# Pass two of a gated spectral/GEGLU training step: accumulators by halves, scratch in blocks, gate gradient as columns, last row tile half by half

## The chip, the cores and the metric

One core of a Trainium2 chip. The metric is the device time of one execution in microseconds (us), lower is better. Each kernel was run several times in rounds in which kernels alternate on the same chip; medians are quoted. A ratio is the mean time of one kernel's fast runs over that of the other's fast runs of the same rounds, so it is not quite the ratio of the medians beside it. "Same" means within 2%.

## The reference, cut to what matters

```python
def _fwd_reference(A_x, A_w_r, A_w_i, B_x, B_w_gate, B_w_up, B_w_down, gate_w):
    x = A_x                                              # [1, 2048, 576] bf16
    g = _sigmoid((x * gate_w).sum(-1, keepdims=True))
    a = _A_ref(x, A_w_r, A_w_i)                          # irfft2(rfft2(x) * W)
    b = _B_ref(x, B_w_gate, B_w_up, B_w_down)            # (gelu(x@wg) * (x@wu)) @ wd, F = 4608
    return g * a + (1 - g) * b
# reference(): this output and, by vjp with grad_out, the gradients of x, w_r, w_i, w_gate, w_up, w_down, gate_w
```

Pass one of the kernel runs the FFTs as matmuls, forms the hidden activation A and its two gradients dHg and dHu, the weight gradients, and stores A, dHg and dHu to scratch in DRAM. Pass two reads the scratch back transposed and contracts over F = 4608, in 36 chunks of 128: a "b" job makes one row tile of the FFN output from A and w_down; a "g" and a "u" job together make one row tile of the input gradient from dHg, w_gate, dHu and w_up. There are 16 row tiles, so 48 jobs of 72 matmuls.

## The kernel before

The parts that matter here (cuts marked with "..."):

```python
scr = [[dram.tile([TPB, P, FF], BF16, name=f"scr{k}_{tp}") for tp in range(NT)] for k in range(3)]
# pass one stores 128 rows of 256 elements at a row pitch of 4608 elements
LD.dma_start(scr[k][tp][:, :, fsl].rearrange("t p f -> p t f"), tl[:])
...
p2in = ctx.enter_context(tc.tile_pool(name="p2in", bufs=6, side="right", **kw))
def pin(k, t, f0):                       # one transposing DMA: 128 rows x 1536 columns; three per job
    tl = p2in.tile([P, FCB, P], BF16, tag="pin", name="pin")
    LD.dma_start_transpose(tl[:], scr[k][t // TPB][t % TPB][:, f0 * P:(f0 + FCB) * P])
    return tl

jobs = [("g", t) for t in range(3)] + [("b", t) for t in range(8)] + [("u", t) for t in range(3)] + [("b", 8)]
for t in range(3, T):
    jobs += [("g", t), ("u", t)] + ([("b", t + 6)] if t + 6 < T else [])
...
tc.tile_pool(name="pacc", bufs=4, space=PSUM, **kw) as pacc      # four accumulators of two banks
def b_job(t):
    bps = pacc.tile([P, 2, 512], F32, tag="acc", name="acc")
    ...
    for f0 in range(0, NFC, FCB):
        At = loaded.pop((0, t, f0))
        for r in range(FCB):
            fc = f0 + r
            for h in range(2):
                nc.tensor.matmul(bps[:, h, :288], lhsT=At[:, r, :], rhs=wd_all[:, fc, h * 288:(h + 1) * 288],
                                 start=(fc == 0), stop=(fc == NFC - 1))
        used[0] += 1
        ensure()                          # issues the next pin, six ahead
    nc.scalar.copy(bo[:].rearrange("p (h d) -> p h d", h=2), bps[:, :, :288])
    ...
def gate_grad():                          # 32 matmuls of 288 columns, one useful row
    for h in range(2):
        for t in range(T):
            nc.tensor.matmul(gps[:, h, :288], lhsT=dlog_bc[:, t, :], rhs=xn[:, t, h * 288:(h + 1) * 288], ...)
def x_end(t):
    ...
    nc.scalar.copy(xo[:].rearrange("p (h d) -> p h d", h=2), xps[:, :, :288])
    V.scalar_tensor_tensor(t1_[:], gwf[:], dlog[:, t:t + 1], xo[:], op0=ALU.mult, op1=ALU.add)
    V.tensor_tensor(o1[:], t1_[:], dxa_t[:], op=ALU.add)
    ST.dma_start(o1v[:, t, :], o1[:])     # ST is the POOL queue, LD the SP queue
for i, (kind, t) in enumerate(jobs):
    if i > 1 and wT_loads:
        load_wuT(*wT_loads.pop(0))        # six transposing loads of w_up, one per job from the third on
```

## Time and profile before

| | value | where from |
|---|---|---|
| time | 1493.64 us median (1491.71 to 1495.65, 4 runs) | runs |
| span of the profiled run | 1490.4 us | page |
| TensorE busy | 97% | page, part 1 |
| pass two, first matmul to last | 1045.33 to 1483.51 us | timeline of TensorE |
| lost between the first b job and the first u job | 10.75 us of 81.31 | timeline of TensorE |
| from the last matmul to the end | 6.9 us | timeline |

The profile lines stand in the prediction.

### The profile page before, as it was taken

The page shows a single profiled execution, that of the slowest core. Times are in us where ns is not written, and L with a number is a line of the kernel's source. Part 1 is how long each engine was busy: PE and PEld are TensorE (multiplying, and loading weights), DVE is VectorE, ACT ScalarE, POOL GpSimd, SP SyncE. Part 2 cuts the span into 40 slices and gives each one's busy share as a digit, 9 for nine tenths or more (in the row PEclk, how much of TensorE's full clock was granted, in tenths as well). Part 3 has the DMA queues.
Part 4 walks back from the last instruction along what each step waited for, and adds up shares of the span by engine and source line. Part 5 has one row for each costly group of instructions (what it writes and reads, how often), then busy time and mean ns, then how long its engine had stood idle before and what let it go on. Part 6 is the DMA issues. An engine that isn't in the chain of part 4 may idle for free.

```text
span 1490.4 us, 29909 instructions
## 1 busy us (share of the span) xinstructions
PE 1450.0 (97%) x11760; PEld 1071.2 (72%) x11760; DVE 843.6 (57%) x2243; ACT 698.2 (47%) x1355; POOL 22.3 (1%) x51
## 2 busy tenths in 40 slices
PE   7889999899999999999999999999998999999998
PEld 5657776666777677677677677778876777777776
DVE  7597766878888887776776776773023211212001
ACT  5576666567667766676666666662000000000000
POOL 1000000000000000000000000000000000000000
PEclk9999999999999999999999999999999999999999
DMA  5144334535444535443444544657999977878772
GB/s 187 42 136 120 91 113 143 148 106 149 135 136 130 147 104 145 128 117 110 128 117 117 149 116 117 163 133 184 245 214 213 187 156 167 162 157 171 150 153 63
DMA packets 503355, 210.49 MB, mean 141 GB/s; under 512 B 307595, under 2 KB 497068, under 8 KB 503212
## 3 DMA queue, kind: packets, MB, share of 16 engines
q1 hardware_dynamic: 499772, 202.83, 55.5%
q0 software_dynamic: 1632, 4.72, 1.2%
q8 instruction: 92, 1.51, 0.5%
q10 hardware_dynamic: 1808, 1.02, 0.2%
q14 instruction: 51, 0.42, 0.1%
HBM read 40.89 MB, written 93.82 MB: 90 GB/s over the span
## 4 chain that ended last, share of the span: by engine, by line
PE 66%; issue 23%; DVE 2%; SPq 1%; ACT 1%; DMA 1%; POOL 1%; POOLq 0%; ACTq 0%; DVEq 0%
PE wps L432 16%; PE xy L332 16%; PE wps L415 9%; PE z L320 8%; PE acc L914 3%; PE wps L445 2%; PE xy L327 2%; PE acc L956 2%; PE pf L671 2%; PE z L323 1%; PE pf L659 1%; PE pf L482 1%; POOL out_dram L971 1%; POOL out_dram L924 0%; DMA scr_p<-Vt 0%
## 5 line engine op out<-in xcount | busy, mean ns | idle before, releaser
L332 PE MATMUL xy<-wgu,xT 128*128 128x512 bf16 x1152 | 271.5, 380 | 0.0
L956 PEld LDWEIGHTS <-pin 128*128 128x128 bf16 x2304 | 225.4, 98 | 56.8
L432 PEld LDWEIGHTS <-xn 128*128 128x128 bf16 x2304 | 225.4, 98 | 32.4 <-issue 0.2
L332 PEld LDWEIGHTS <-xT 128*128 128x128 bf16 x1152 | 106.9, 98 | 137.9 <-issue 31.0
L345 ACT ACTIVATE da<-z,omg 128x256 bf16<-128x256 f32 x288 | 113.0, 475 | 154.1 <-PE z L323 154.0
L415 PE MATMUL wps<-dB,A 128*128 128x288 bf16 x1152 | 154.2, 286 | 0.0
L914 PE MATMUL acc<-wd_all,pin 128*128 128x288 bf16 x1152 | 145.4, 288 | 7.9 <-DMA pin<-scr 4.2
L320 PE MATMUL z<-wdT,dOT 128*128 128x256 bf16 x1152 | 140.2, 276 | 5.9 <-ACT Vt L622 4.1
L956 PE MATMUL acc<-wuT,pin 128*128 128x288 bf16 x1152 | 143.4, 286 | 0.0
L956 PE MATMUL acc<-wgT,pin 128*128 128x288 bf16 x1152 | 143.4, 286 | 0.0
L914 PEld LDWEIGHTS <-pin 128*128 128x128 bf16 x1152 | 113.3, 98 | 38.6 <-DMA pin<-scr 4.8
L415 PEld LDWEIGHTS <-A 128*128 128x128 bf16 x1152 | 112.7, 98 | 35.7
L432 PE MATMUL wps<-dHg,xn 128*128 128x256 bf16 x1152 | 134.4, 273 | 0.0
L432 PE MATMUL wps<-dHu,xn 128*128 128x256 bf16 x1152 | 131.5, 273 | 0.0
L320 PEld LDWEIGHTS <-dOT 128*128 128x128 bf16 x1152 | 112.6, 99 | 24.2 <-issue 9.6
L966 ACT COPY f32t<-acc 128x576 f32<-128x576 f32 x16 | 10.2, 639 | 249.1 <-PE acc L956 249.1
L351 ACT ACTIVATE q<-xy 128x512 bf16<-128x512 f32 x144 | 86.0, 597 | 73.0 <-PE xy L332 69.4
L968 DVE SCALAR_TENSOR_TENSOR f32t<-gwf,dlog,f32t 128x576 f32<-128x576 f32 x16 | 13.1, 818 | 186.9 <-ACT f32t L966 186.9
L358 DVE TENSOR_SCALAR s<-q 128x512 bf16<-128x512 bf16 x144 | 41.8, 290 | 107.9 <-ACT q L351 106.1
L367 ACT ACTIVATE om<-s 128x512 bf16<-128x512 bf16 x144 | 92.1, 640 | 6.9 <-DVE s L359 6.6
L368 ACT ACTIVATE s<-s 128x512 bf16<-128x512 bf16 x144 | 90.7, 630 | 4.6
L919 ACT COPY f32t<-acc 128x576 f32<-128x576 f32 x16 | 10.2, 640 | 172.0 <-PE acc L914 172.0
(176 smaller groups left out, 1819.8 us busy)
## 6 DMA issues: line engine op xcount, KB each, us to landing
scr<-A SPq DMA_DIRECT2D x144, 128.0 KB, 1.8
scr<-dHg SPq DMA_DIRECT2D x144, 128.0 KB, 1.9
scr<-dHu SPq DMA_DIRECT2D x144, 128.0 KB, 1.9
out_dram<-dw SPq DMA_DIRECT2D x67, 128.0 KB, 1.9
wd_all<-in_B_w_down_dram SPq DMA_DIRECT2D x3, 1728.0 KB, 12.0
out_dram<-dwd SPq DMA_DIRECT2D x34, 144.0 KB, 1.9
scr_p<-Vt SPq DMA_DIRECT2D x32, 144.5 KB, 2.3
Vp<-scr_p SPq DMA_DIRECT2D x16, 289.0 KB, 3.2
```

Source lines behind the costliest of these rows:

```text
L320: nc.tensor.matmul(zo(t), lhsT=dOT[:, ci, t, :], rhs=wdT[:, ci, :], start=(t % 4 < 2 and ci == 0), stop=False)
L327: nc.tensor.matmul(xy[t % 4 // 2][:, t % 2, :], lhsT=xT[r, 4, t, :], rhs=wgu[r, 4, :], start=True, stop=False)
L332: nc.tensor.matmul(xy[k][:, t % 2, :], lhsT=xT[:, ci, t, :], rhs=wgu[:, ci, :], start=False, stop=(ci == 3))
L345: nc.scalar.activation(da[:, tt, :], z[:, tt, k, :], ACT.Copy, scale=omg32[:, t:t + 1])
L351: nc.scalar.activation(q[:], xy[:, :, 0:FG], ACT.Square)
L358: V.tensor_scalar(s[:], q[:], A_GELU, 1.0, op0=ALU.mult, op1=ALU.add)
L367: nc.scalar.activation(om[:], s[:], ACT.Sigmoid, scale=-2.0 * C_GELU)
L368: nc.scalar.activation(s[:], s[:], ACT.Sigmoid, scale=2.0 * C_GELU)
L415: nc.tensor.matmul(wps[:, :288], lhsT=tl(0, t)[:, fch * P:(fch + 1) * P], rhs=dB[:, t, h * 288:(h + 1) * 288], start=(t == 0), stop=(t == ...
L432: nc.tensor.matmul(wps[:, cc, :], lhsT=xn[:, t, (c0 + cc) * P:(c0 + cc + 1) * P], rhs=tl(k, t), start=(t == 0), stop=(t == T - 1))
L914: nc.tensor.matmul(bps[:, h, :288], lhsT=At[:, r, :], rhs=wd_all[:, fc, h * 288:(h + 1) * 288], start=(fc == 0), stop=(fc == NFC - 1))
L956: nc.tensor.matmul(xps[:, h, :288], lhsT=src[:, r, :], rhs=wT[:, h * 288:(h + 1) * 288], start=(k == 1 and f0 + r == 0), stop=(k == 2 and ...
```

## The change

Four parts. Accumulators become single PSUM banks (eight of them), with the two halves of D one after the other, so that one half is copied out while the other is computed. The scratch is stored in blocks of 128 x 256 that a transposing DMA reads as one contiguous run. The gate gradient is made as columns: 80 matmuls with one column each. The last row tile is done half by half, the first half stored beside the second half's matmuls, from the SP queue.

```diff
-    scr = ... dram.tile([TPB, P, FF], BF16, ...)
+    scr = ... dram.tile([TPB, NG, P, FG], BF16, ...)
-            LD.dma_start(scr[k][tp][:, :, fsl].rearrange("t p f -> p t f"), tl[:])
+            LD.dma_start(scr[k][tp][:, g].rearrange("t p f -> p t f"), tl[:])
...
+        tl = p2in.tile([P, FCH, FCB // FCH, P], BF16, tag="pin", name="pin")
+        src = scr[k][t // TPB][t % TPB, g0:g0 + FCB // FCH].rearrange("g p f -> (g p) f")
+        LD.dma_start_transpose(tl[:].rearrange("q c g p -> q c (g p)"), src)
...
-         tc.tile_pool(name="pacc", bufs=4, space=PSUM, **kw) as pacc:
+         tc.tile_pool(name="pacc", bufs=8, space=PSUM, **kw) as pacc:
...
+                for h in range(2):
+                    block(bps[h], h, At, lambda r: wd_all[:, f0 + r], f0 == 0, f0 + FCB == NFC)
+                    if f0 + FCB == NFC:
+                        nc.scalar.copy(bo[:, h * 288:(h + 1) * 288], bps[h][:, :288])
...
+            for c in range(5):
+                n = min(P, D - c * P)
                 for t in range(T):
+                    nc.tensor.matmul(gps[0:n, c:c + 1], lhsT=xn[:, t, c * P:c * P + n], rhs=dlog_bf[:, t:t + 1], ...)
...
+                ST.dma_start(out_7[0:512].rearrange("(c p) -> p c", p=P), dgw[:, 0:4])
+                ST.dma_start(out_7[512:D].rearrange("(p o) -> p o", o=1), dgw[LO, 4:5])
...
+        def x_last(t):
+            ...
+            for h in range(2):
+                for k, f0, src in srcs:
+                    block(accs[t][h], h, src, wT(k, f0), k == 1 and f0 == 0, k == 2 and f0 + FCB == NFC)
+                x_out(t, h, pre, o1, LD)      # one DVE add out of PSUM, store from SP
```

More of the change, by code (lines that the diff above doesn't have):

```diff
@@ L198 @@
     o5v = out_5[0:512, :].rearrange("(c p) f -> p c f", p=P)
-    scr = [[dram.tile([TPB, P, FF], BF16, name=f"scr{k}_{tp}") for tp in range(NT)] for k in range(3)]
+    scr = [[dram.tile([TPB, NG, P, FG], BF16, name=f"scr{k}_{tp}") for tp in range(NT)] for k in range(3)]
     a_scr = dram.tile([S, D], BF16, name="a_scr")
@@ L379, in H_ew2 @@
         V.tensor_tensor(dHu[:], da[:], xb[:], op=ALU.mult)
-        fsl = slice(g * FG, (g + 1) * FG)
         for k, tl in enumerate((A, dHg, dHu)):
-            LD.dma_start(scr[k][tp][:, :, fsl].rearrange("t p f -> p t f"), tl[:])
+            LD.dma_start(scr[k][tp][:, g].rearrange("t p f -> p t f"), tl[:])
         kept.setdefault(g, []).append((A, dHg, dHu))
@@ L850, in pin @@
     def pin(k, t, f0):
-        tl = p2in.tile([P, FCB, P], BF16, tag="pin", name="pin")
-        LD.dma_start_transpose(tl[:], scr[k][t // TPB][t % TPB][:, f0 * P:(f0 + FCB) * P])
+        tl = p2in.tile([P, FCH, FCB // FCH, P], BF16, tag="pin", name="pin")
+        g0 = f0 // FCH
+        src = scr[k][t // TPB][t % TPB, g0:g0 + FCB // FCH].rearrange("g p f -> (g p) f")
+        LD.dma_start_transpose(tl[:].rearrange("q c g p -> q c (g p)"), src)
         return tl
@@ L857 @@
         jobs += [("g", t), ("u", t)] + ([("b", t + 6)] if t + 6 < T else [])
-    seq = [("bgu".index(kind), t, f0) for kind, t in jobs for f0 in range(0, NFC, FCB)]
+    jobs[-2:] = [("x", T - 1)]
+    seq = [(k, t, f0) for kind, t in jobs for k in ((1, 2) if kind == "x" else ("bgu".index(kind),)) for f0 in range(0, NFC, FCB)]
     loaded = {}
@@ L888 @@
          tc.tile_pool(name="p2res", bufs=1, **kw) as p2res, \
-         tc.tile_pool(name="pacc", bufs=4, space=PSUM, **kw) as pacc:
+         tc.tile_pool(name="pacc", bufs=8, space=PSUM, **kw) as pacc:
         wuT = [p2res.tile([P, FCB, D], BF16, name=f"wuT{k}") for k in range(NB)]
         dlog = p2res.tile([P, T], F32, name="dlog")
-        dlog_bc = p2res.tile([P, T, P], BF16, name="dlog_bc")
+        dlog_bf = p2res.tile([P, T], BF16, name="dlog_bf")
         gwf = p2res.tile([P, D], F32, name="gwf")
@@ L901, in b16t, with acc_pair, block, wT @@
             return p2b.tile([P, D], BF16, tag="b16t", name="b16t")
+        def acc_pair():
+            return [pacc.tile([P, 512], F32, tag="acc", name="acc") for _ in range(2)]
+        def block(acc, h, src, w_of, first, last):
+            for r in range(FCB):
+                nc.tensor.matmul(acc[:, :288], lhsT=src[:, r % FCH, r // FCH, :], rhs=w_of(r)[:, h * 288:(h + 1) * 288],
+                                 start=(first and r == 0), stop=(last and r == FCB - 1))
+        def wT(k, f0):
+            return (lambda r: wgT_all[f0 + r]) if k == 1 else (lambda r: wuT[f0 // FCB][:, r])
         def b_job(t):
-            bps = pacc.tile([P, 2, 512], F32, tag="acc", name="acc")
+            bps = acc_pair()
             a_t = b16t()
@@ L908, in b_job @@
             LD.dma_start(do_t[:], do_v[:, t, :])
+            bo = f32t()
             for f0 in range(0, NFC, FCB):
                 At = loaded.pop((0, t, f0))
-                for r in range(FCB):
-                    fc = f0 + r
-                    for h in range(2):
-                        nc.tensor.matmul(bps[:, h, :288], lhsT=At[:, r, :], rhs=wd_all[:, fc, h * 288:(h + 1) * 288],
-                                         start=(fc == 0), stop=(fc == NFC - 1))
+                for h in range(2):
+                    block(bps[h], h, At, lambda r: wd_all[:, f0 + r], f0 == 0, f0 + FCB == NFC)
+                    if f0 + FCB == NFC:
+                        nc.scalar.copy(bo[:, h * 288:(h + 1) * 288], bps[h][:, :288])
                 used[0] += 1
                 ensure()
-            bo = f32t()
-            nc.scalar.copy(bo[:].rearrange("p (h d) -> p h d", h=2), bps[:, :, :288])
             tmpo = f32t()
@@ L932, in b_job @@
             V.tensor_tensor(dlog[:, t:t + 1], dg[:], gg[:], op=ALU.mult)
-            V.tensor_copy(dlog_bc[:, t, :], dlog[:, t:t + 1].to_broadcast([P, P]))
+            V.tensor_copy(dlog_bf[:, t:t + 1], dlog[:, t:t + 1])
         def gate_grad():
-            gps = pacc.tile([P, 2, 512], F32, tag="acc", name="gps")
-            for h in range(2):
+            gps = pacc.tile([P, 512], F32, tag="acc", name="gps")
+            for c in range(5):
+                n = min(P, D - c * P)
                 for t in range(T):
-                    nc.tensor.matmul(gps[:, h, :288], lhsT=dlog_bc[:, t, :], rhs=xn[:, t, h * 288:(h + 1) * 288],
+                    nc.tensor.matmul(gps[0:n, c:c + 1], lhsT=xn[:, t, c * P:c * P + n], rhs=dlog_bf[:, t:t + 1],
                                      start=(t == 0), stop=(t == T - 1))
-            dgw = p2s.tile([1, 2, 288], BF16, tag="dgw", name="dgw")
-            V.tensor_copy(dgw[:], gps[0:1, :, :288])
-            ST.dma_start(out_7.rearrange("(o d) -> o d", o=1), dgw[:].rearrange("o h d -> o (h d)"))
+            dgw = p2s.tile([P, 5], BF16, tag="dgw", name="dgw")
+            V.tensor_copy(dgw[:, 0:4], gps[:, 0:4])
+            V.tensor_copy(dgw[LO, 4:5], gps[LO, 4:5])
+            with nc.allow_non_contiguous_dma(reason="one column of 576 numbers"):
+                ST.dma_start(out_7[0:512].rearrange("(c p) -> p c", p=P), dgw[:, 0:4])
+                ST.dma_start(out_7[512:D].rearrange("(p o) -> p o", o=1), dgw[LO, 4:5])
         accs = {}
@@ L948, in x_half @@
             if k == 1:
-                accs[t] = pacc.tile([P, 2, 512], F32, tag="acc", name="acc")
-            xps = accs[t]
+                accs[t] = acc_pair()
             for f0 in range(0, NFC, FCB):
                 src = loaded.pop((k, t, f0))
-                for r in range(FCB):
-                    wT = wgT_all[f0 + r] if k == 1 else wuT[f0 // FCB][:, r]
-                    for h in range(2):
-                        nc.tensor.matmul(xps[:, h, :288], lhsT=src[:, r, :], rhs=wT[:, h * 288:(h + 1) * 288],
-                                         start=(k == 1 and f0 + r == 0), stop=(k == 2 and f0 + r == NFC - 1))
+                for h in range(2):
+                    block(accs[t][h], h, src, wT(k, f0), k == 1 and f0 == 0, k == 2 and f0 + FCB == NFC)
@@ L958, in x_half, with x_pre @@
                 used[0] += 1
                 ensure()
-        def x_end(t):
-            xps = accs.pop(t)
+        def x_pre(t):
             dxa_t = b16t()
             LD.dma_start(dxa_t[:], dxa_v[:, t, :])
-            xo = f32t()
-            nc.scalar.copy(xo[:].rearrange("p (h d) -> p h d", h=2), xps[:, :, :288])
-            t1_ = f32t()
-            V.scalar_tensor_tensor(t1_[:], gwf[:], dlog[:, t:t + 1], xo[:], op0=ALU.mult, op1=ALU.add)
-            o1 = b16t()
-            V.tensor_tensor(o1[:], t1_[:], dxa_t[:], op=ALU.add)
-            ST.dma_start(o1v[:, t, :], o1[:])
+            pre = f32t()
+            V.scalar_tensor_tensor(pre[:], gwf[:], dlog[:, t:t + 1], dxa_t[:], op0=ALU.mult, op1=ALU.add)
+            return pre
@@ new lines, in x_out, with x_end @@
+        def x_out(t, h, pre, o1, st):
+            hs = slice(h * 288, (h + 1) * 288)
+            V.tensor_tensor(o1[:, hs], accs[t][h][:, :288], pre[:, hs], op=ALU.add)
+            st.dma_start(o1v[:, t, hs], o1[:, hs])
+        def x_end(t):
+            pre = x_pre(t)
+            o1 = b16t()
+            for h in range(2):
+                x_out(t, h, pre, o1, ST)
+            accs.pop(t)
+        def x_last(t):
+            accs[t] = acc_pair()
+            pre = x_pre(t)
+            o1 = b16t()
+            srcs = [(k, f0, loaded.pop((k, t, f0))) for k in (1, 2) for f0 in range(0, NFC, FCB)]
+            for h in range(2):
+                for k, f0, src in srcs:
+                    block(accs[t][h], h, src, wT(k, f0), k == 1 and f0 == 0, k == 2 and f0 + FCB == NFC)
+                x_out(t, h, pre, o1, LD)
@@ L979 @@
                 x_half(t, 1)
-            else:
-                if t == T - 1:
-                    gate_grad()
+            elif kind == "u":
                 x_half(t, 2)
                 x_end(t)
+            else:
+                gate_grad()
+                x_last(t)
 _INS = ['A_x', 'A_w_r', 'A_w_i', 'B_x', 'B_w_gate', 'B_w_up', 'B_w_down', 'gate_w', 'grad_out']
```

## The prediction

> **What bounds the kernel now.** I read the page first, then the timeline of TensorE from 1030 us on, then the timeline of the SP queue over the same stretch, then the DMA strips of short windows, and last the final 8 us. The page says TensorE is busy nearly always:
>
> ```profile
> PE 1450.0 (97%) x11760; PEld 1071.2 (72%) x11760; DVE 843.6 (57%) x2243; ACT 698.2 (47%) x1355; POOL 22.3 (1%) x51
> ```
>
> The change touches pass two alone (from 1045.33 us, the first matmul of line 956), except for the address at which pass one stores its scratch. So the question is where, in pass two, TensorE does not issue. The timeline of TensorE (start, duration, instructions, and in brackets the idle time before and what ended it) shows it:
>
> ```profile
> 1071.78 8.98 PE L914 MATMUL acc<-wd_all,pin 128*128 128x288 bf16 x72
> 1081.49 8.98 PE L914 MATMUL acc<-wd_all,pin 128*128 128x288 bf16 x72 [0.73 <-ACT f32t L919]
> ...
> 1121.83 10.67 PE L914 MATMUL acc<-wd_all,pin 128*128 128x288 bf16 x72 [2.15 <-DMA pin<-scr]
> 1134.51 8.99 PE L914 MATMUL acc<-wd_all,pin 128*128 128x288 bf16 x72 [2.02 <-DMA pin<-scr]
> 1144.28 8.98 PE L914 MATMUL acc<-wd_all,pin 128*128 128x288 bf16 x72 [0.77 <-ACT f32t L919]
> ...
> 1188.37 8.98 PE L956 MATMUL acc<-wgT,pin 128*128 128x288 bf16 x72
> 1197.19 8.98 PE L956 MATMUL acc<-wuT,pin 128*128 128x288 bf16 x72
> ...
> 1470.61 4.08 PE L939 MATMUL gps<-xn,dlog_bc 128*128 128x288 bf16 x32
> 1474.53 8.98 PE L956 MATMUL acc<-wuT,pin 128*128 128x288 bf16 x72
> ```
>
> See that undisturbed jobs of 72 matmuls start 8.82 us apart (1197.19 less 1188.37), 122.5 ns each, and that between 1153 and 1470 us there is no gap at all. All loss lies in the eight first "b" jobs, 1071.78 to 1153.09 us: 81.31 us where 8 x 8.82 = 70.56 would do, so **10.75 us**. Starts that are 9.71 to 9.77 apart lose some 0.9 each to the wait for the one free accumulator (three "g" tiles hold the other three), and two starts lose 2.3 and 3.9 to the wait for a transposed scratch tile; the job at 1121.83 also ran 1.69 us long, at a granted clock of 0.71 in the window 1124 to 1128.
>
> Why is the tile late? The SP queue issues everything in order, and from 1064.65 us on it never rests:
>
> ```profile
> 1098.68 4.69 SPq L879 DMA_TRANSPOSE wuT<-in_B_w_up_dram  x1
> 1103.42 0.57 SPq L906 DMA_DIRECT2D b16t<-a_scr  x1
> 1104.04 0.43 SPq L908 DMA_DIRECT2D b16t<-in_grad_out_dram  x1
> 1104.57 6.29 SPq L852 DMA_TRANSPOSE pin<-scr  x3
> 1110.91 4.74 SPq L879 DMA_TRANSPOSE wuT<-in_B_w_up_dram  x1
> ```
>
> One job's share of this queue is 4.7 + 1.1 + 6.3, about 12.1 us, against 8.82 us of TensorE. The stage is bound by transposing DMA until the six wuT loads are through; the PSUM waits only use up time that the DMA would otherwise have charged.
>
> The end, after the last matmul, is the last part that sets the time:
>
> ```profile
> 1483.55 0.64 ACT L966 COPY f32t<-acc 128x576 f32<-128x576 f32 x1 [20.92 <-PE acc L956]
> 1484.22 0.82 DVE L968 SCALAR_TENSOR_TENSOR f32t<-gwf,dlog,f32t 128x576 f32<-128x576 f32 x1 [8.75 <-ACT f32t L966]
> 1485.08 0.76 DVE L970 TENSOR_TENSOR b16t<-f32t,b16t 128x576 bf16<-128x576 f32 x1
> 1486.13 0.58 POOL L971 DMA_DIRECT2D out_dram<-b16t  x1 [9.83 <-DVE b16t L970]
> ```
>
> The matmuls end at 1483.51, the span at 1490.4: **6.9 us** of copy, two vector operations, a store from POOL and closing.
>
> **What the Trainium skill says.** "TensorE: Matmul & The Clock Gate", section "Wait — 56ns, not 53.3ns?", gives N/2.4 GHz plus about 2.5 ns from start to start, and a floor near 25 ns for small N. The trace agrees: 122.5 ns for 288 columns, and the 80 one-column matmuls of the gate in pass one took 2.14 us, 26 ns each with their weight loads. "PSUM — Partial Sum Buffer", section "PSUM bank collisions raise a hardware error", asks to guard PSUM by bank; so one half can be copied out while the other bank is written, and the 0.73 us waits are the whole two-bank copy. "DMA: Bandwidth & Descriptors", section "Latency and other measured facts", has DMA transposes at 261 GB/s with a non-contiguous middle dimension and 350 to 400 when contiguous, which speaks for the block layout; the trace shows a plateau of 289 GB/s for every transpose, never 350, with slow stretches near 130. The same section gives a shorter first byte to hardware queues than to software ones (0.6 against 1 us); the trace has 3.0 us to landing for stores from POOL and 1.8 to 1.9 from SP.
>
> **The change part by part.** (1) Single-bank accumulators, halves one after the other. The half-0 copy now runs beside the 12 matmuls of half 1 (12 x 122.5 ns = 1.47 us). A 16-element ACT operation took 184 ns and the 576-element copy 640, so a 288-element copy is about 0.40 us by interpolation: hidden. This removes all the 0.9 us waits, five before the first DMA wait or merged with it, one at 1144.28. Matmul and weight-load counts do not change (each matmul had its own load before, 11760 of both on the page), so the order of halves costs TensorE nothing. But if the DMA is no faster, the job at 1121.83 still starts when its tile lands, and so does the one at 1134.51; the four earlier waits become a longer DMA wait of about 6 us (1121.83 less 1071.78 + 5 x 8.82). Then only the wait at 1144.28 is gained: **0.95 us**. If the DMA is fast enough all 10.75 us are.
> (2) Scratch in blocks. Same bytes, same 256 B packets, same 144 transposes. The tile is now 768 rows of 256 elements, contiguous, where it was 128 rows of 1536 at a pitch of 9216 bytes. To clear both DMA waits, the tiles at 1121.83 and 1134.51 must come 5.9 and 9.8 us earlier (the second: 1134.51 less 1071.78 + 6 x 8.82 = 1124.7). Between 1064.65 and 1134.5 about 38 us of the queue are pin tiles, so they must be about a quarter faster: 1.5 us each in place of 2.05. At the plateau, 393 KB at 289 GB/s take 1.36 us, so there is room, if the slow stretches go. The stores in pass one keep 512 B pieces and lie beside TensorE: 0.
> (3) Gate gradient as columns. 32 matmuls of 122.5 ns (3.92 us) become 80 of one column at 26 ns (2.1 us), on the path: **1.8 us**. The scattered store of 576 numbers starts some 17 us before the end and is hidden.
> (4) Last row tile by halves. Half 0 is added and stored beside half 1's 72 matmuls. After the last matmul remain one DVE addition out of PSUM (759 ns for 578 elements elsewhere, so 0.41 us for 288), about 0.1 of hand-over, a store from SP of 1.9 us to landing, and some 0.8 us of closing: 3.2 us where it was 6.9, so **3.7 us**. gwf*dlog+dxa is made ahead.
> Sum: 0.95 + 1.8 + 3.7 = 6.45 us with the DMA as it is, 10.75 + 1.8 + 3.7 = 16.25 us with the DMA out of the way.
>
> **The rivals.** *Rival A: the PSUM waits only turn into DMA waits*, since tiles in blocks transpose no faster. For it: the transposes of the same row form in pass one (wgT, 576 rows of 256 columns) show alone the same start of about 0.9 us at 75 to 240 GB/s before the plateau as a pin tile alone, and the loads of w_down, with a pitch of 1152 bytes only, do so too. Time 1486.2. *Rival B: the blocks fix the transposes.* For it: the wuT transposes, 576 rows at the same pitch, hold the plateau where pin tiles beside them fall to half. These are the strips of 1124 to 1128 us (wuT) and 1128 to 1132 us (pins), 0.1 us a slice:
>
> ```profile
> GB/s 287 300 292 289 287 289 259 262 253 215 182 212 177 205 218 161 269 292 292 289 287 287 287 294 287 294 292 289 289 294 292 289 287 287 287 294 287 294 292 293
> GB/s 146 113 169 184 311 254 138 138 230 369 380 337 142 92 64 108 141 131 110 128 125 143 148 156 264 294 287 292 292 294 289 287 247 164 279 97 154 169 169 133
> ```
>
> Many rows per transpose may be what keeps it at 289. Time 1476.4. *Rival C: something gets slower*: transposes of 768 rows that cost more, a pair of banks handed out so that half 0 waits on half 1's copy (about 0.5 us for each of seven jobs, hidden under A), or the 6 us pause that drops the clock once more for longer. Time 1488 to 1492.
>
> **Range and chances.** A gets about one half, B or something between A and B 0.4, C 0.1. The weighted time is 0.5 x 1486.2 + 0.4 x 1480 + 0.1 x 1490 = 1484.1; I take 1484.0. The low end, 1475.5, is all of B and 1 us of luck; the high end, 1489, a mild C. Over 2% would be 30 us, nearly twice the whole sum, so faster gets 0.02; slower needs pass one to be hurt by the new store addresses, 0.02.
>
> **What would show it.** In the profile of after: no wait of TensorE for ACT in the first b jobs (part 1 right); waits for pin of some 6 us at the sixth b job and 2 at the seventh (A), or none, with three pin tiles issued in about 4.5 us where it was 6.3 (B). The one-column matmuls of the gate gradient last about 2.1 us (3), and the span ends about 3.2 us after the last matmul (4). TensorE still starts undisturbed jobs 8.82 us apart. The prediction is wrong if pass two starts at another time than near 1045 us, if one job takes over 8.9 us, or if the end is above 5 us.

## The result, and the profile after

Median 1486.41 us (1485.53 to 1488.09, 4 runs) against 1493.64 us; ratio 0.9953, 95% interval 0.9936 to 0.997. That is "same", some 7 us faster. A control run of the same kernel in later rounds gave 0.9962 (0.9947 to 0.9978).

The page's first part, the timeline of TensorE and the windows of the last tile, for the changed kernel:

```profile
PE 1449.1 (98%) x11808; PEld 1070.9 (72%) x11808; DVE 843.1 (57%) x2260; ACT 690.3 (47%) x1355; POOL 30.5 (2%) x66
```

```profile
1071.63 35.44 PE L912 MATMUL acc<-wd_all,pin 128*128 128x288 bf16 x288
1107.32 8.99 PE L912 MATMUL acc<-wd_all,pin 128*128 128x288 bf16 x72 [0.25 <-DMA pin<-scr]
1117.89 8.99 PE L912 MATMUL acc<-wd_all,pin 128*128 128x288 bf16 x72 [1.57 <-DMA pin<-scr]
1129.93 19.23 PE L912 MATMUL acc<-wd_all,pin 128*128 128x288 bf16 x144 [3.05 <-DMA pin<-scr]
1149.00 26.62 PE L912 MATMUL acc<-wuT,pin 128*128 128x288 bf16 x216
...
1457.70 2.34 PE L953 MATMUL gps<-dlog_bf,xn 128*128 128x1 bf16 x80
1459.97 6.26 PE L912 MATMUL acc<-wgT,pin 128*128 128x288 bf16 x36
1466.07 4.57 PE L912 MATMUL acc<-wuT,pin 128*128 128x288 bf16 x36
```

The first four b jobs now run without a break: the waits for ACT are gone. Waits for pin tiles are 4.87 us in all, with 1.4 us more lost to slow matmuls after the longest (144 matmuls took 19.23 where 17.8 would do). The stretch from the first b job to the first u job is 1149.00 less 1071.63, **77.4 us where it was 81.3**. After the gate's 80 matmuls, 36 matmuls took 6.10 us (1466.07 less 1459.97) where 4.41 is normal. The windows (us, busy times, then the granted clock, DMA share, GB/s) show why:

```profile
1460.00:1461.00 1.00, 1.00 (x9) 0.76 (x8) 0.00 (x0) 0.00 (x0) 0.00 (x0) 0.78 0.27 12
1461.00:1462.00 1.00, 1.00 (x6) 0.63 (x5) 0.00 (x0) 0.00 (x0) 0.00 (x0) 0.50 1.29 303
1462.00:1463.00 1.00, 1.00 (x6) 0.60 (x4) 0.03 (x1) 0.00 (x0) 0.00 (x0) 0.50 0.79 247
```

The granted clock was 0.50. The same lines have TensorE busy all the time (1.00 in the sum): busy time cannot show this.

The end, in the timeline:

```profile
1471.16 9.85 SPq L985 DMA_DIRECT2D out_dram<-b16t  x2
1474.89 4.57 PE L912 MATMUL acc<-wuT,pin 128*128 128x288 bf16 x36
1480.19 0.46 DVE L984 TENSOR_TENSOR b16t<-acc,f32t 128x288 bf16<-128x288 f32 x1 [9.05 <-PE acc L912]
```

Half 0 is stored from 1471.16 on beside half 1's matmuls, and the last addition takes 0.46 us. But the last recorded matmul ends at 1479.46 and the addition starts at 1480.19, 0.7 us later (0.04 us in the kernel before). The span ends at 1484.4.

Where the 6.0 us between the two traces (1490.44 and 1484.41) came from:

| stretch | before | after | gain |
|---|---|---|---|
| up to the first matmul of pass two | 1045.33 | 1045.17 | 0.16 |
| first b job to first u job | 81.31 | 77.38 | 3.9 |
| first u job to the start of the last matmul | 330.14 | 330.17 | 0.0 |
| from there to the end | 7.20 | 5.24 | 2.0 |

The three g jobs in between take 26.45 us in both. One trace is one draw: pass two began anywhere between 1044.9 and 1047.9 us in these runs. And of the kernel before there is one trace alone.

### The profile page after: what moved, and what is told of

It is laid out like the page before. It is cut to its first block, busy times and chain, and to the rows that moved or that the text cites. A ratio compares the mean times of both kernels' runs of the same rounds, so it can differ in the third digit from the quotient of the medians.

```text
span 1484.4 us, 30047 instructions
## 1 busy us (share of the span) xinstructions
PE 1449.1 (98%) x11808; PEld 1070.9 (72%) x11808; DVE 843.1 (57%) x2260; ACT 690.3 (47%) x1355; POOL 30.5 (2%) x66
## 4 chain that ended last, share of the span: by engine, by line
PE 90%; DVE 2%; DMA 2%; ACT 1%; SPq 1%; issue 0%; ACTq 0%
PE acc L912 28%; PE wps L431 17%; PE xy L332 16%; PE wps L414 9%; PE z L320 8%; PE wps L444 2%; PE xy L327 2%; PE pf L670 2%; PE z L323 2%; PE pf L658 1%; DMA pin<-scr 1%; PE pf L481 1%; DMA scr_p<-Vt 0%; ACT xb L356 0%; DVE Vt L501 0%
## 5 line engine op out<-in xcount | busy, mean ns | idle before, releaser
L930 ACT COPY f32t<-acc 128x288 f32<-128x288 f32 x32 | 12.6, 400 | 315.1 <-PE acc L912 304.8
L979 DVE SCALAR_TENSOR_TENSOR f32t<-gwf,dlog,b16t 128x576 f32<-128x576 f32 x16 | 13.1, 817 | 237.0 <-DMA b16t<-dxa_scr 237.0
L359 DVE TENSOR_TENSOR s<-xb,s 128x512 bf16<-128x512 bf16 x144 | 61.3, 425 | 51.5 <-ACT xb L356 46.5
L357 ACT CAST hu<-xy 128x512 bf16<-128x512 f32 x144 | 86.9, 603 | 0.0
```

The costliest lines, as they stand in the source:

```text
L357: nc.scalar.copy(hu[:], xy[:, :, FG:2 * FG])
L359: V.tensor_tensor(s[:], xb[:], s[:], op=ALU.mult)
```

## The experiments

All started from the changed kernel unless said otherwise, all gave correct results, and all were timed against the kernel before in the same rounds. "Stretch" is first b job to first u job; "tail" is from the end of the last recorded matmul to the end of the span.

| run | edit | median us (before) | ratio, 95% interval | stretch | tail |
|---|---|---|---|---|---|
| (changed kernel) | | 1486.41 (1493.64) | 0.9953, 0.9936-0.997 | 77.4 | 4.95 |
| e12_after_again | none | 1487.28 (1493.24) | 0.9962, 0.9947-0.9978 | 80.4 | 5.54 |
| e1_strided | no blocks | 1489.95 (1492.94) | 0.9981, 0.9967-0.9995 | 79.3 | 6.66 |
| e2_pair | two-bank tiles | 1496.33 (1492.94) | 1.0021, 1.0008-1.0033 | 80.5 | 6.55 |
| e8_pair_one_copy | two-bank tiles, one copy | 1493.67 (1494.74) | 0.9993, 0.9978-1.0009 | 81.7 | 7.95 |
| e7_act_loads | row loads on the ACT queue | 1493.57 (1494.74) | 0.999, 0.9971-1.0008 | 78.1 | 8.04 |
| e6_wuT_spread | w_up loads spread, twelve b jobs first | 1484.52 (1494.74) | 0.9931, 0.9917-0.9944 | no loss | 7.22 |
| e3_gate_rows | gate as rows | 1486.8 (1492.94) | 0.9961, 0.9949-0.9974 | 77.8 | 3.81 |
| e4_gate_spread | gate columns spread | 1491.33 (1492.94) | 0.9987, 0.9975-1.0 | 77.1 | 3.79 |
| e9_gate_row_store | gate stored as rows | 1486.91 (1494.74) | 0.995, 0.9938-0.9963 | 80.3 | 3.37 |
| e10a_gate_best | e4 + e9 | 1484.77 (1493.24) | 0.9943, 0.993-0.9956 | 76.8 | 3.37 |
| e10_best | e4 + e9 + e6 | 1478.38 (1493.24) | 0.9897, 0.9884-0.9911 | no loss | 3.36 |
| e13_best_strided | e10_best, no blocks | 1483.13 (1492.86) | 0.9939, 0.9925-0.9953 | 0.5 lost | 3.37 |

The first theory was the prediction's: pass two's first b jobs are bound by transposing DMA, waits for PSUM and for DMA fill the same time, and the blocks made the DMA somewhat faster. Its rival: the freed banks gave the gain by themselves.

### Blocks undone

```diff
-    dram.tile([TPB, NG, P, FG], ...)          # store, read and lhsT slices as before the change
+    dram.tile([TPB, P, FF], ...)
```

> The changed kernel with its scratch rows strided again (128 rows of 1536 elements per transpose), all else as changed. Measure: the stretch from the first matmul of the first b job to the first of the first u job, 81.3 us before, 77.4 us after. Theory (transposing DMA bounds this stretch and the blocks made it faster): three pin tiles need about 6.2 us of the queue again where the blocks needed 5.6, and the stretch grows to 80 to 81 us, since only one PSUM wait was really gained; the whole run about 3 us longer than the changed kernel. Rival (the 3.9 us came from the freed banks, blocks are idle show): the stretch stays at 77 to 78 us and the time as changed.

Stretch 79.3 us, between the two expectations; time 1489.95 us, 0.9981. Six traces with the changed code in this stretch have 76.8, 77.1, 77.4, 77.8, 80.3 and 80.4 us (mean 78.3), so one trace cannot tell 79.3 from them. By time, undoing the blocks costs about 0.2 to 0.3% against the two sets of the changed kernel, with intervals that overlap. What the traces do show is a burst of pins alone: the first six, issued in a row at the end of pass one, took 13.4 and 13.1 us of the SP queue with strided scratch before and here, and 11.0 to 11.6 us in the traces with blocks of these rounds. In the crowded stretch too the two layouts stand apart: the 21 pins of the second to the eighth b job took 42.2 and 41.1 us of the queue with strided rows (before and here), 37.6 to 40.0 us in the eight traces with blocks and the same issue order. So the blocks do make the pins faster, by some 7%; what that is worth in time, this run does not settle. See the last one.

### Single banks undone, twice

```diff
-            return [pacc.tile([P, 512], F32, ...) for _ in range(2)]     # bufs=8
+            two = pacc.tile([P, 2, 512], F32, ...)                       # bufs=4
+            return [two[:, 0], two[:, 1]]
```

> The changed kernel with the two halves of an accumulator in one two-bank tile out of four, so that the next b job waits until both halves are copied; blocks, order of halves and the rest as changed. Theory (DMA bounds the stretch): waits of 0.5 to 0.7 us for ACT come back at the first b jobs, but the later waits for pin tiles shrink by as much, so the stretch first b to first u is 77.5 to 78.5 us (77.4 as changed) and the time grows by under 1 us. Rival (freed banks gave the 3.9 us): the stretch is 80 to 81.5 us and the time grows by 3 us or more.

Stretch 80.5 us, which looks like the rival, but the run did more than it should: each b job waited twice, 0.49 us for the copy of half 0 ahead of its own half 1 (the two halves are now one tile) and 0.49 us again for the next job, so jobs stood 10.16 us apart, more than in the kernel before. No wait for pins was left at that pace. So far the waits exchange, as the theory says. The mended version copies both halves at once, as before the change:

```diff
-                    if f0 + FCB == NFC:
-                        nc.scalar.copy(bo[:, h * 288:(h + 1) * 288], bps[h][:, :288])
+            nc.scalar.copy(bo[:].rearrange("p (h d) -> p h d", h=2), two[:, :, :288])   # after the loop
```

> The changed kernel with two-bank accumulators (four of them) and one copy of both halves after the last matmul, as before the change; blocks, order of halves and all else as changed. This mends the earlier pair run, in which a copy of half 0 also held up half 1. Theory (PSUM waits and DMA waits fill the same time): each of the first eight b jobs starts 9.7 us after the last, so the stretch from the first b job to the first u job is 8 x 9.7 = 77.7 us, hardly more than the 77.4 of the changed kernel, and the waits for pin tiles vanish or fall under 1 us in all. Rival (the waits add up): the pin waits of 4.9 us stay and the stretch is 81 us or more.

The timeline of TensorE in that run:

```profile
1101.19 8.98 PE L913 MATMUL acc<-wd_all,pin 128*128 128x288 bf16 x72 [0.77 <-ACT f32t L932]
1110.94 8.98 PE L913 MATMUL acc<-wd_all,pin 128*128 128x288 bf16 x72 [0.77 <-ACT f32t L932]
1121.83 8.99 PE L913 MATMUL acc<-wd_all,pin 128*128 128x288 bf16 x72 [1.91 <-DMA pin<-scr]
1133.79 10.37 PE L913 MATMUL acc<-wd_all,pin 128*128 128x288 bf16 x72 [2.97 <-DMA pin<-scr]
1144.93 8.98 PE L913 MATMUL acc<-wd_all,pin 128*128 128x288 bf16 x72 [0.77 <-ACT f32t L932]
```

By its numbers this looks like the rival: the waits for pins stay (1.91 + 2.97 = 4.88 us, as in the changed kernel's 4.87), the waits for ACT come on top, and the stretch is 81.7 us, that of the kernel before. But the waits can only add up if TensorE holds up the SP queue, which issues the pins. Here are the three pins of the sixth b job, first in the changed kernel, then in this one:

```profile
1113.98 5.51 SPq L854 DMA_TRANSPOSE pin<-scr  x3
```

```profile
1117.50 5.45 SPq L854 DMA_TRANSPOSE pin<-scr  x3
```

Counted from the first b job (1071.63 and 1072.02) they are issued at 42.4 and 45.5 us: later, so something slowed the queue. In the stretch 1064 to 1143 us the SP queue's own waits (in total, times, longest) were, in the kernel before and in the changed one:

```profile
SPq L852 <- PE acc L914: 11.3, 10, 1.8
```

```profile
SPq L854 <- PE acc L912: 17.9, 16, 1.9
```

This view seems to say that the queue waits for TensorE to give back one of six pin buffers. It did not. The buffers go round, so a pin takes the buffer of the sixth pin before it: the first pin of the sixth job takes that of the first pin of the fourth job, and the fourth job here starts at 1101.19 and has read that pin after 24 of its matmuls, at 1104.3 us. The new pin is issued at 1117.50, 13.2 us later (12.8 in the changed kernel). In these three traces each of the 21 pins of the second to the eighth b job was issued 0.1 to 14.4 us after its buffer had come free, and the pauses between the queue's instructions, from the first w_up load to the first u job's pins, add up to 3.4 us of 74 to 79. Where the queue does wait for a buffer, before and after this stretch, it issues 0.03 us after the release. The view books a part of a transpose's own time as a wait when TensorE signals while it runs. And e2_pair, whose TensorE waited 7.6 us for ACT in this stretch, issued the sixth job's pins at 42.0 us, not later.

What differs from trace to trace is how long the transposes themselves take on the queue (the six w_up pieces and the 21 pins):

| traces | 27 transposes, us | sixth job's pins issued, us | stretch, us |
|---|---|---|---|
| before: strided, two-bank | 68.9 | 45.1 | 81.3 |
| e1_strided: strided, single banks | 68.7 | 44.2 | 79.3 |
| e8_pair_one_copy: blocks, two-bank | 67.3 | 45.5 | 81.7 |
| e9, e12: blocks, single banks | 67.3, 67.5 | 44.5, 44.7 | 80.3, 80.4 |
| changed, e3, e4, e10a: blocks, single banks | 64.3, 64.6, 63.9, 64.9 | 42.4, 42.8, 42.0, 42.1 | 77.4, 77.8, 77.1, 76.8 |

The same code gives stretches of 77 or of 80 us, by how fast its transposes went. The run with two-bank tiles drew a slow queue; the 77.7 us of the theory had reckoned with the fast one. Beside traces of like queue time, the single banks are worth 1.4 us (81.7 against 80.3 and 80.4) and 2.0 us (81.3 against 79.3): an estimate from single traces. So the waits mostly exchange. Why the same transposes take 64 us in one run and 67 in another, no trace here says. By time, e8_pair_one_copy is 0.3 to 0.4% slower than the changed kernel; 2.4 to 3.0 us of that lie in its tail, which the copy of the b jobs does not touch.

### Is it the data or the queue?

```diff
-            LD.dma_start(a_t[:], a_v[:, t, :])            # and do_t
+            nc.scalar.dma_start(a_t[:], a_v[:, t, :])
```

> The changed kernel with the two plain row loads of each b job issued from the ACT queue in place of SP, so that each job's share of the SP queue shrinks by 1.1 us and the bytes stay. Theory (the data rate binds, the SP queue only backs up behind it): stretch 76.5 to 77.5 us where it was 77.4, time within 1 us of the changed kernel. Rival (issuing on the one queue binds): some 5 us less, stretch about 72 us, no waits for pins.

The stretch was 78.1 us, far from the rival's 72: taking 1.1 us of issuing per job off the SP queue gained nothing, since the 27 transposes now took 72.5 us of it (64.3 in the changed kernel). So issuing the rows is not the limit, the transposes are. The time, 1493.57 us, is 7 us worse than the changed kernel's and was not expected; in the trace the tail is 8.0 us, with the last store 6.7 us from issue to the SP queue's drain. What else the slower runs lost (1489.26 to 1495.91 us) is not known.

```diff
-    jobs = g0..g2, b0..b7, u0..u2, b8, ...
+    jobs = g0..g2, b0..b11, u0..u2, b12, ...
-            if i > 1 and wT_loads:
+            if i > 1 and i % 2 == 0 and wT_loads:
```

> The changed kernel with twelve b jobs ahead of the first u job in place of eight, and the six transposing loads of w_up spread over every other job in place of every job. Same work in all. Theory (the stretch is bound by the bytes that transposing DMA has to bring per job): per job 1.18 MB of pins, 0.44 of w_up and 0.44 of plain rows need about 2.06 MB in 8.82 us, 234 GB/s, near what the queue gave; the waits for pin tiles fall from 4.9 us with a slow-clock stretch behind them to under 2 us in all, and the time falls by 4 to 6.5 us, to about 0.9915 of before. Rival (tiles are late for want of buffers or for the latency of each transpose): waits of over 4 us stay and the time is as changed.

```profile
1074.34 106.17 PE L912 MATMUL acc<-wd_all,pin 128*128 128x288 bf16 x864
```

Twelve b jobs, 864 matmuls, without a single wait: 106.0 us from the first b to the first u job, where 12 x 8.82 = 105.8 are the least. The theory of the amount per job holds: the same bytes on the same queue with the same buffers, only not six w_up transposes in six consecutive jobs (the four further b jobs make the room for that; the two edits were not tried apart). Ratio 0.9931. But the tail was 7.2 us, so something at the end still cost.

### The gate gradient

```diff
-    80 matmuls: lhsT=xn[:, t, chunk], rhs=dlog_bf[:, t:t + 1]   -> one column each
+    32 matmuls: lhsT=dlog_bc[:, t, :], rhs=xn[:, t, half]       -> 288 columns each
```

> The changed kernel with the gate gradient as rows again: 32 matmuls of 288 columns in place of 80 of one column, at the same place before the last row tile. Theory (the one-column matmuls leave the array so idle that its clock is halved after them, which costs the 1.7 us that were won): the gate takes 3.9 us, no granted clock under 0.9 follows, the first 36 matmuls of the last tile take 4.4 us where they took 6.1, and the end is within 0.5 us of the changed kernel's. Rival (the slow matmuls have another cause, such as the last tiles landing late): the slow matmuls stay and the run is 1.7 us longer than the changed kernel.

```profile
1460.38 4.08 PE L952 MATMUL acc<-xn,dlog_bc 128*128 128x288 bf16 x32
1464.30 4.57 PE L912 MATMUL acc<-wgT,pin 128*128 128x288 bf16 x36
```

The gate takes 3.9 us again, the 36 matmuls after it 4.41, the granted clock is 1.00, and first u job to last matmul is 330.14 us, to a few hundredths that of the changed kernel (330.17). The theory holds: 1.65 us won by short matmuls, 1.69 lost to the clock. The slow clock does not come each time. Of eight traces with 80 one-column matmuls right before the last tile, four show it (the changed kernel, its control, e6_wuT_spread and e9_gate_row_store), four do not. Which four, the clock records of the traces tell. Within a trace, all changes of the granted clock lie whole multiples of 3.41 us apart (in the changed kernel at 1129.5, 1132.9, 1460.6 and 1464.0 us). In the four traces with the slow clock the 80 matmuls, 2.2 us long, lay inside one such step (they began 0.28 to 0.79 us after its start), and the clock fell at its end; in the four without it they began 1.35 to 2.80 us after a step's start and ran over into the next. So whether the cost came was chance, which no edit here controlled.

The warning stood in the kernel before. Its pass one makes the gate by 80 one-column matmuls too, at 52.05 to 54.19 us, where the prediction read its 26 ns; at 54.50 the clock fell to 0.50, though TensorE had not paused in that step. In eight of the 14 traces these 80 lay inside one step, and in all eight the clock fell at its end. In the other six it fell a step later, when TensorE had paused as well. Counting the columns that the recorded matmuls of a step stream (some 8,000 in a full one), every step at full clock with under 2,880 was followed by the half clock and none with over 3,420, in all 14 traces; in between, some were and some were not.

It also came out that the tail is 1.1 us shorter with rows, 3.81 us.

The columns again, now in groups among full matmuls:

```diff
-                gate_grad()              # all 80 before the last tile
+                gate_part(c)             # 16 after each of five jobs, the result stored two jobs earlier
```

> The changed kernel with the 80 one-column matmuls in five groups of 16, each after one of the last five jobs before the last tile, so that full matmuls stand on both sides of every 0.42 us. Theory (halved clock after a long low-activity stretch): no granted clock under 0.9, 36 matmuls take 4.4 us, the sum of the gate stays 2.1 to 2.3 us, and the time is 1.7 to 2.4 us shorter than the changed kernel's, 1484 us or so against before at 1493.6. Rival (not the clock of the low-activity stretch): slow matmuls still come at the last tile and the time stays as changed.

No slow clock followed the groups and the tail was 3.8 us, as the theory said, yet the time was 4 to 5 us worse than the changed kernel's:

```profile
1468.62 4.55 PE L912 MATMUL acc<-wgT,pin 128*128 128x288 bf16 x24 [6.65 <-DMA pin<-scr]
```

The last tile waits 6.65 us for a pin, and in that wait the clock fell after all (0.50 from 1464.8 to 1471.6 us), so its 24 matmuls took 4.55 us and not 3.1. The landing times of DMA in 1444 to 1470 us (size, median us from issue to landing) show what came in between:

```profile
pin<-scr SPq DMA_TRANSPOSE x5, 10.5
out_dram<-dgw POOLq DMA_DIRECT2D x1, 1.0 KB, 19.1
```

The store of the gate gradient as columns, 512 pieces of 2 bytes in 1 KB, takes 19 us, and pins behind it take up to 18 us where 4.0 is the median. In the changed kernel the same store goes out at 1465.7 us, when no pin is left to delay. But it delays the row stores there. So the next run changed that alone:

```diff
-                ST.dma_start(out_7[0:512].rearrange("(c p) -> p c", p=P), dgw[:, 0:4])   # and 64 more
+            nc.tensor.transpose(rps[0:4, 0:P], dgw[:, 0:4], ident[:])                    # after half 0; [LO, 4:5] likewise
+            V.tensor_copy(dgr[:, 0, :], rps[0:4, 0:P])
+            LD.dma_start(out_7[0:512].rearrange("(c p) -> c p", p=P), dgr[:, 0, :])      # 4 pieces of 256 B, 1 of 128
```

> The changed kernel with the gate-gradient columns turned into rows by two small transposes on TensorE after half 0 of the last tile, and stored in five pieces of 256 or 128 bytes from SP, in place of 576 pieces of 2 bytes from POOL. The 80 one-column matmuls stay where they are. Theory S (the scattered store keeps the DMA busy for some 17 us and delays what comes after it): the POOL drain of 17 us is gone, the last store takes 2.0 us or less to landing, half 0's store about 2 us in place of 11. Theory L (the late finish of TensorE, 0.7 us after the last recorded matmul in the changed kernel, 1.6 in the strided one and 0.04 where the gate was rows, comes from the store too): the finish is 0.04 us late. Rival of L (it comes from the clock after the one-column matmuls): slow matmuls and late finish together still cost 1.5 to 2.4 us. Time 0 to 2 us less than the changed kernel.

```profile
1463.78 6.25 PE L912 MATMUL acc<-wgT,pin 128*128 128x288 bf16 x36
...
1479.05 4.57 PE L912 MATMUL acc<-wuT,pin 128*128 128x288 bf16 x36
1483.66 0.46 DVE L995 TENSOR_TENSOR b16t<-acc,f32t 128x288 bf16<-128x288 f32 x1 [8.52 <-PE acc L912]
```

The clock still drops (6.25), so the store has nothing to do with that. The last addition now starts 0.04 us after the last matmul, and the tail is 3.37 us. POOL's last drains in the changed kernel and here (ns, least, median and most):

```profile
L1043 POOLq DRAIN  x3: 40/102/16976, 1466.2 to 1484.1; - x3
```

```profile
L1056 POOLq DRAIN  x3: 40/93/4576, 1469.1 to 1486.7; - x3
```

From 17.0 to 4.6 us. Theory S holds. Theory L holds for the most part: of the seven traces with the scattered store shortly before the end, six show TensorE finishing 0.55 to 1.95 us after its last recorded matmul and one (e7_act_loads) 0.04; of the six without it there (e3, e9, e10a, e10 and e13, and e4, which issued it 41 us before the end), none shows more than 0.05. How a store can make TensorE finish late stays open. The total time did not follow (0.995): this profiled run lost 80.3 us in the stretch, which the edit does not touch.

### The control, and the mends together

> The changed kernel unaltered, as a control in the same rounds as the next two, and for a second trace of it. Expected from the first: ratio to before 0.995 to 0.996; the stretch from the first b job to the first u job between 77 and 80.5 us, as the four traces with this code in that stretch had 77.1 to 80.3. If the scattered store of the gate gradient disturbs the end, the tail after the last recorded matmul is again over 4.5 us (3.4 with the row store), and the POOL drain about 17 us.

As expected in all points: ratio 0.9962, stretch 80.4 us, clock halved again, tail 5.54 us. The stretch alone swings by 3 us from run to run.

> The changed kernel with both mends of the gate gradient: its one-column matmuls in five groups of 16 between full jobs, and its result turned into rows on TensorE and stored in five pieces, not 576. Theory (the gate's gain of 1.8 us was eaten by the half clock after 80 one-column matmuls in a row, and the tail's by the scattered store): no half clock at the last tile, tail 3.4 to 3.8 us, waits for pins at the end none; from the last u job's reckoning 2 to 3.5 us less than the changed kernel of the same rounds. Rival (both effects are noise of single traces): same time as the changed kernel, within 0.7 us.

The edit is that of e4_gate_spread and e9_gate_row_store together. 1484.77 against the control's 1487.28 us in the same rounds, 2.5 us less; the intervals of the ratios overlap a little, so by time this is likely rather than sure. By trace, from the first u job to the end: 330.17 + 5.83 = 336.0 us in the control, 328.89 + 3.65 = 332.5 us here. No half clock, no wait for pins at the end, tail 3.37 us.

> The last kernel with the w_up transposes spread over every other job and twelve b jobs ahead of the first u job. All three causes found are mended: no waits for pins in the first b jobs (0.2 us in all where the changed kernel lost 6.8), no half clock, tail 3.4 to 3.8 us. Expected sum against the changed kernel of the same rounds: 6.6 for the stretch and 2 to 3.5 for the gate, 8.5 to 10 us less; about 1478 us where before has 1494, ratio to before 0.989 to 0.990. Rival (the gains hide one another): no better than the w_up spread alone, 0.993.

```profile
1073.94 106.00 PE L912 MATMUL acc<-wd_all,pin 128*128 128x288 bf16 x864
...
1469.10 4.57 PE L912 MATMUL acc<-wuT,pin 128*128 128x288 bf16 x36
1473.71 0.46 DVE L1000 TENSOR_TENSOR b16t<-acc,f32t 128x288 bf16<-128x288 f32 x1 [8.36 <-PE acc L912]
```

1478.38 us, ratio 0.9897, 9 us less than the control in the same rounds and 15 less than the kernel before: it beats both kernels, clear of the intervals. The gains do not hide one another: against the control's ratio e6_wuT_spread alone is 0.31% better, e10a_gate_best alone 0.19%, both together 0.65%.

> The fastest kernel so far (gate mended, w_up spread) with its scratch strided again, to see what the block layout is worth where the w_up transposes no longer crowd the queue. Six pin transposes in a row took 13.1 to 13.4 us of the SP queue with strided scratch (two traces) and 11.0 to 12.5 with blocks (ten traces). Theory (blocks are some 15% faster and that is needed): a job's three pins, half a w_up piece and plain rows take 6.6 + 2.2 + 1.1 = 9.9 us with strided scratch against 8.8 with blocks, so the twelve b jobs wait for pins, 3 to 8 us in all, and the ratio to before is 0.992 to 0.995 in place of 0.990. Rival (the queue's backlog, not the layout, was the cost): no waits, ratio 0.990 as with blocks.

Ratio 0.9939 as the theory had it, with an interval clear of that of e10_best (0.9884 to 0.9911), though the two ran on different chips. Its six runs spread from 1477.03 to 1484.88 us, those of e10_best from 1477.19 to 1479.0. The profiled run was the fastest of the six and shows a wait of 0.36 us only, not the 3 to 8 expected; its first six pins took 11.6 us, not 13. Its 21 pins of the second to the eighth b job took 40.5 us of the queue, against 36.5 in e10_best. So the blocks are worth some 4 to 6 us (means of all runs, and ratios), and strided scratch can, now and then, be as good. Where the slower runs lose it, no trace here shows.

## Why the prediction was right or wrong

The time (1484.0 predicted, 1486.41 measured) lay in the range, and close to its rival A (1486.2). But A's sum came out by errors that cancel, and it should not be taken as confirmed.

**What bounds the kernel: right.** That the loss lies in the b jobs beside the six w_up transposes is right; spreading them removed all of it (e6_wuT_spread, e10_best). "From 1064.65 us on it never rests" holds for the stretch too: the pauses of the queue add up to 3.4 us of 79, and no pin waited for its buffer. One slip: the 3.9 us that the start at 1134.51 loses hold the 1.69 us by which the job before ran long; the wait itself is 2.02.

**Part 1: the mechanism was right, its size small.** Jobs start when their tile lands, and the waits for PSUM mostly filled time that the DMA would have charged. The single banks were worth 1.4 to 2.0 us beside traces of like queue time (an estimate), where 0.95 was forecast. The copy of half 0 hidden beside half 1 was right (no wait for ACT left; 400 ns for 288 elements against the 0.40 us interpolated).

**Part 2, the step that failed: rival A's "tiles in blocks transpose no faster".** They were faster, though not by the quarter of rival B. The 21 pins took 38.7 us of the queue in place of 42.2, 1.84 us each for 2.01. Counted from the first b job, the sixth job could start 3.8 us earlier (46.3 for 50.1) and the seventh 4.4 (58.3 for 62.7), where B needed 5.9 and 9.8. So the waits for pins were 0.25, 1.57 and 3.05 us at the fifth to the seventh job, where A expected some 6 and 2 at the sixth and the seventh and B none, and the stretch gained 3.9 us in the first trace (3.0 by the mean of six: 81.3 less 78.3), between A's 0.95 and B's 10.75. As the same code swings from 76.8 to 80.4 us, a part of it can be the draw of the trace. The waits for pins went only where the w_up loads were spread out.

**Part 3: the instruction cost was right, its worth wrong.** 2.27 us for 3.92, near the 1.8 us forecast (1.65). The missing term is the clock: in four traces of eight it fell to 0.50 for 3.4 us and took 1.69 us back, and whether it did was chance. And the scattered store "starts some 17 us before the end and is hidden" failed: it occupied the DMA for some 17 us, up to the end.

**Part 4: mis-sized in the changed kernel by the neighbour, right by itself.** Predicted tail 3.2 us, measured 4.95 and 5.54 us (the prediction had named an end above 5 us as a sign of being wrong); without the scattered store 3.36 to 3.81. So the gain was 2.0 us in the first trace and 1.4 in the control, in place of 3.7, and 3.5 once the store was mended.

So A's 0.95 + 1.8 + 3.7 = 6.45 was in truth 3.9 + 0.0 + 2.0, and 0.16 from pass one: 6.0. Rivals A and B both left out that two of the change's own parts, the columns and the half-by-half end, would meet.

## What to carry to other kernels

When a view says that a queue waits for another engine, look up when the thing waited for came free: here the buffers had been free for up to 14 us, and the "wait" was the transfers' own time. And where the same code swings by 3 us from trace to trace, a single trace of an edit can agree with a rival to the number by chance; compare it with traces in which the queue was as slow. Short matmuls in a row and stores in 2-byte pieces have costs that fall on their neighbours (half clock for the next 3.4 us, 17 to 19 us of slow DMA); spread the first between full ones, and turn columns into rows on TensorE before storing them. A load needed only later, spread over more jobs, was worth about as much here as all four parts of the change (6.4 us, e10_best against e10a_gate_best, for 6 to 7).

## What the Trainium skill lacked or had wrong

- "TensorE: Matmul & The Clock Gate", Part 1: the half clock is told of idle gaps; that a run of one-column matmuls, with no gap between them, can bring it on is not there. Here 80 of them in 2.27 us were followed by a granted clock of 0.50 for 3.4 us in the four traces where they lay inside one step of the clock's changes, and by none in the four where they ran over its end, nor where they came in groups of 16.
- "DMA: Bandwidth & Descriptors", Specifications: it says that transfers under 512 B are below line rate and read-modify-write. It doesn't say how much one such store holds up: 1 KB in 2-byte pieces landed after 19.1 us, and transposes beside it took up to 18 us where 4.0 is the median.
- The same page, "Latency and other measured facts": 350 to 400 GB/s for contiguous DMA transposes. No run here shows that: a pin of contiguous blocks alone on the DMA has a plateau of 287 to 294 GB/s (changed kernel, 1404.6 to 1405.3 us), that of the strided one (289), and the DMA as a whole moved 223 GB/s in the crowded stretch of the changed kernel (209 before).
- No page tells that TensorE can finish 0.55 to 1.95 us after its last recorded matmul; six of seven traces with the scattered store do, none of six without. The cause is open.
